# A retention and gated-MLP kernel: two accumulators swapped, two scalings shared between VectorE and GpSimd, and two small steps moved to VectorE

## The chip, the cores and the metric

The kernel runs on one core of one Trainium2 chip. The core has five engines, each with its own instruction queue: TensorE (PE in the profile; its weight loads are shown apart as PEld), VectorE (DVE), ScalarE (ACT), GpSimd (POOL) and SyncE (SP), which here only issues DMAs. TensorE's products go to accumulators in PSUM, which VectorE and ScalarE read and copy to the on-chip memory SBUF. The metric is the device time of one execution in microseconds (us); lower is better.

## The reference

```python
def _attn_ref(q, k, v):                      # (8, 8, 576, 64): batch, head, position, width
    scores = scale * np.matmul(q, k.transpose(0, 1, 3, 2))
    gamma = 1.0 - 2.0 ** (-5.0 - np.arange(H))
    rel = pos[:, None] - pos[None, :]
    Dmat = np.where(rel >= 0, gamma[:, None, None] ** rel[None], 0.0)
    return np.matmul(scores * Dmat[None], v)

def _moe_ref(x, w_in, w_out, beta):          # x (4608, 512), w_in (512, 2048), w_out (2048, 512)
    h = x @ w_in
    g = h * (1.0 / (1.0 + np.exp(-beta * h)))
    return g @ w_out
```

The attention's output, heads side by side, is `x` of the second part. All inputs and the output are float32.

## The kernel before

**Retention.** The decay `gamma ** (i - j)` is split into a factor for each query row and one for each key row. `pre_q` multiplies q by `gq`; v is multiplied by `gv` or `gvh`, and keys are copied to bf16. Within a piece of positions the causal product is computed directly: scores on TensorE, a mask on VectorE (`R`), then mask times v (`O`). What comes from earlier pieces goes through a state, the running sum of key times v, kept in float32 by additions on VectorE (`sums`) and in bf16 (`sbds`, `sbq`, `ends`) for TensorE. The output in PSUM, `O`, is copied to `xT` in bf16, transposed so that it can be the moving side of the next product.

**MLP.** For each block of 512 rows, `up`, `ups` and `first_ups` compute `w_in` times `xT` into an accumulator `ph`, from which ScalarE makes `gT` with a Silu scaled by beta; `down` multiplies `gT` by `w_out` (already divided by beta) into `po`, which is copied to `ot` and stored.

**Batches.** Of the 576 positions of a batch, 512 form a block; the last 64 of all batches are put together into one more block. Batches 0 and 1 work in two spans of 256 positions each, and their queries and keys are transposed on TensorE (`t_q`, `s_T`, `o_T`). From batch 2 on, DMAs transpose them. Batch 0's retention stands ahead of everything else, in an order written out by hand (the `s_` functions). Here `s_keep` copies states, `s_cross` multiplies them by queries, `s_x` copies `O` to `xT`, and `ups` then starts the first `up`.

**Order.** From there on, `fill` is a list of TensorE's MLP steps. Streams of other steps have a due time each, in places of `fill`, and `merged` emits a step when its due time is reached. `d0` is the place of batch 0's first `down`, `u1` that of batch 1's first `up`. Batch 1's retention is prepared by `pre_q(1, n)`, `o_pre(span, j, a)` (j = 0 keys, j = 1 v; a is the half of the heads) and `o_T`, and done by `first_span`, `first_out`, `second_span` and `second_out`. `first_out` calls `o_out(0)`, which computes the outputs of span 0 and, between its products, the second state with `o_st(1)`; it copies the outputs, transposes the keys of span 1 (`o_T(1)`) and adds up the state (`o_keep(1)`).

**Accumulators.** PSUM is handed out by tag: three "mm", two "O", two "sc", one "st". The planner gives a new tile one of its tag's buffers and makes its first writer wait until the old tile's readers are done. `phs[0]` and `phs[1]` of `first_ups` are "mm", and so is the `ph` of each `up` that follows (L703).

**Beta.** `betas` brings beta into rows on TensorE. `betas_safe` adds 1e-12 where beta squared is below 1e-24, so that its reciprocal exists; it is used by every Silu and by the scaling of `w_out`.

Of the kernel before, what the change touches and what calls it, by code (L numbers as in the profile page):

```python
# [19 lines left out]
def kernel(  # L20
# [10 lines left out]
    nc = tc.nc  # L31
# [219 lines left out]

    def betas_safe():

        nc.gpsimd.tensor_tensor(tiny[:], beta_sb[:], beta_sb[:], ALU.mult)
        nc.gpsimd.tensor_scalar(tiny[:], tiny[:], 1e-24, 1e-12, ALU.is_lt, ALU.mult)
        nc.gpsimd.tensor_tensor(beta_sb[:], beta_sb[:], tiny[:], ALU.add)

# [18 lines left out]
    def pre_q(b, n):  # L278

        if n == 0:  # L280
            batch[b] = dict(qs=sb.tile([P, CB, H, D], BF16, name="qs", tag="qs", bufs=2),
                            qT=sb.tile([P, CB, HP, P], BF16, name="qT", tag="qT", bufs=2))
        if b < 2:
            hs, cs = slice(n // 2 * HP, (n // 2 + 1) * HP), slice(n % 2 * 2, n % 2 * 2 + 2)
            for to, hs in [(hs, hs)] if n < 2 or b < QB else turned[1:]:
                nc.vector.tensor_tensor(batch[b]["qs"][:, cs, to], q_tiles[b][:, hs, cs].rearrange("p h i d -> p i h d"),
                                        gq[:, cs, hs].unsqueeze(3).to_broadcast([P, 2, len(range(H)[hs]), D]), ALU.mult)
        else:
            if n % 2:
                return  # L290
            cs = slice(n, n + 2)
            for to, hs in turned:
                nc.gpsimd.tensor_tensor(batch[b]["qs"][:, cs, to], q_tiles[b][:, hs, cs].rearrange("p h i d -> p i h d"),  # L293
                                        gq[:, cs, hs].unsqueeze(3).to_broadcast([P, 2, len(range(H)[hs]), D]), ALU.mult)
# [62 lines left out]
    def span_of(b, s):  # L357
        if (b, s) not in spans:
            spans[b, s] = dict(kn=sb.tile([P, 2, H, D], BF16, name="kn", tag="kn", bufs=4),
                               kT=sb.tile([P, 2, HP, P], BF16, name="kT", tag="kT", bufs=4),  # L360
                               vn=sb.tile([P, 2, H, D], BF16, name="vn", tag="vn", bufs=VB), R={})
        return spans[b, s]
# [61 lines left out]
    def s_x(a, hh, e):  # L424
        e(xt(0)[:, 2 * a:2 * a + 2].rearrange("k p i (s h w) -> k (p i) s h w", s=2, h=2)[:, :, :, hh, :],  # L425
          s_Os[a][hh].rearrange("k s p (i w) -> k (p i) s w", i=CB))
# [20 lines left out]
    def s_keep(a, n, es, bank=None, at=None):  # L447

        ps, at = slice(2 * a, 2 * a + 2), 2 * a if at is None else at
        for j in range(2):  # L450
            st = s_sts[min(n, 1) if bank is None else bank][half(j), at:at + 2, half(j)]
            if n < 3:
                es[j](sbds[n][half(j), ps, half(j)], st)  # L453
            else:
                es[j](ends[0][half(1 - j if a else j), ps], st)
# [104 lines left out]
        return lambda: cross(1), evict  # L560


    def o_pre(s, j, a, e=None):

        w, S, e = slice(a * HP, (a + 1) * HP), span_of(1, s), e or nc.gpsimd
        src = span_tiles[1, s, j].rearrange("p h i d -> p i h d")
        if j:
            e.tensor_tensor(S["vn"][:, :, w], src[:, :, w],
                            gvh[:, 2 * s:2 * s + 2, w].unsqueeze(3).to_broadcast([P, 2, HP, D]), ALU.mult)
            return  # L570
        for to, hs in turned[1:] if a else turned[:1]:
            e.tensor_copy(S["kn"][:, :, to], src[:, :, hs])  # L572

    def o_T(s, tags, es):

        S, ts = spans[1, s], []
        for a in range(2):
            if a < len(tags):
                T = psum.tile([P, 2 // len(tags), 2, 2, P], BF16, name="T", tag=tags[a], bufs=3 if tags[a] == "mm" else 2)
            t = T[:, a if len(tags) == 1 else 0]  # L580
            for i in range(2):
                for pl in range(2):
                    nc.tensor.transpose(t[:, i, pl, :], heads(S["kn"][:, i], 2 * a + pl), ident[:])
            ts.append(t)
        for a in range(2):
            es[a](S["kT"][:, :, 2 * a:2 * a + 2], ts[a])
# [19 lines left out]
                    nc.vector.tensor_tensor(S["R"][a][:, j], sc[a][j][:], causal_span[:].unsqueeze(2).to_broadcast([P, 2, 2, P]), ALU.mult)  # L606
        return masks

    def o_st(c):

        S, hh = spans[1, c // 2], c % 2
        st = psum.tile([P, HP, D], F32, name="st", tag="st", bufs=1)
        for i in range(2):
            for p in range(HP):
                for j in range(2):
                    nc.tensor.matmul(st[half(j), p, :], S["kn"][half(hh), i, 2 * p + j, :], S["vn"][half(hh), i, head_of(1, p, j), :],
                                     start=i == 0 and p == 0, stop=True, skip_group_check=True)
        return st
# [12 lines left out]
    def o_out(s):  # L631

        S, seen = spans[1, s], set()
        O = {(hh, y): psum.tile([P, 2, P], F32, name="O", tag="sc" if y else "O", bufs=2) for y in range(2) for hh in range(2)}

        def to(hh, p, x):
            first, o = (hh, p // 2, x) not in seen, O[hh, p // 2][half(x), p % 2, :]
            seen.add((hh, p // 2, x))
            return o, first

        def own(hj):
            for i in range(2):
                for pp in range(2):
                    for y in range(2):
                        for hh, j in hj:
                            p = pp + 2 * y
                            h = head_of(1, p, j)
                            o, first = to(hh, p, h % 2)
                            m = nc.tensor.matmul(o, S["vn"][half(hh), i, h, :], S["R"][y][half(hh), j, i, pp, :],  # L649
                                                 start=first, stop=True, skip_group_check=True)  # L650
                            held_back.append(m)
            return m

        def cross(cj):
            for pp in range(2):
                for y in range(2):
                    for hh, j in cj:
                        c, p = 2 * s + hh, pp + 2 * y
                        o, first = to(hh, p, j ^ y)
                        m = nc.tensor.matmul(s_view(o), sbq[2 * c - 1][half(j), p, :], o_q(c, half(j), p),  # L660
                                             start=first, stop=True, skip_group_check=True)
                        held_back.append(m)
            return m

        def fence(last):
            f = nc.vector.memset(fenced[:], 0.0)
            after(f, last)
            held_back.clear()
            return f

        held_back = []
        if s == 0:
            f = fence(cross([(1, 0), (1, 1)]))
            st = o_st(1)
            own([(0, 0), (0, 1), (1, 1)])
            held_back.clear()
            own([(1, 0)])
        else:
            f = fence(own([(0, 1), (1, 0)]))
            own([(0, 0), (1, 1)])  # L680
            st = o_st(3)
            cross([(0, 0), (1, 1)])
            held_back.clear()
            cross([(0, 1), (1, 0)])
        for m in held_back[:2 + 2 * s]:
            after(m, f)

        def evict():
            for n, ((hh, y), o) in enumerate(O.items()):
                c = 2 * s + hh  # L690
                (dve, act)[n % 2](xt(1)[:, 2 * y:2 * y + 2, :, c * PC:(c + 1) * PC], o.rearrange("k p (i w) -> k p i w", i=CB))
        return evict, st
# [75 lines left out]
    def F(f, *a):  # L768
        return lambda: f(*a)
# [3 lines left out]

    warm_up(2, MB)
    betas()
    betas_safe()
    pre_q(0, 0)
    pre_q(0, 1)
    t_q(0, 0)
# [36 lines left out]
    s_x(0, 0, act)  # L816
    s_cross(3, 0)
    s_st(1, 1, 0, low)
    s_x(0, 1, act)
    s_keep(1, 0, (dve, dve), 1)  # L820
    s_st(1, 0, 1, low)
    s_keep(1, 2, (dve, dve), 0)
    s_O(0, 1, "sc")
    s_O(1, 1, "sc")
    cast_w_in(0, (0, 1), (1,))
    cast_w_in(1, (0, 1), (1,))
    cast_w_in(0, (2, 3), (3,))
# [63 lines left out]
    def first_out():  # L891
        evict, st = o_out(0)
        evict()
        o_T(1, ("mm",), (act, dve))
        o_keep(1, st)

    def second_span():
        masks = o_sc(1)
# [9 lines left out]
    def triangles():  # L908
        for t, pattern in zip(tri, ([[1, CB], [CB, TL // CB]], [[1, TL]])):
            nc.gpsimd.memset(t[:], 1.0)  # L910
            for x in range(2):
# [11 lines left out]
                (d0 + 13.6, F(x_k, XB, 0)),  # L923
                (base[2] - 4.5, F(release, 4)), (base[2] + 10, F(release, 4))],
               [(d0 + 7, F(pre_q, 1, n)) for n in range(4)] + [(d0 + 12.5, F(pre_q, XB, n)) for n in range(4)] + [(d0 + 11.6, F(t_q, 1, 0)), (d0 + 11.6, F(t_q, 1, 1))],
               [(d0 + 8, F(o_pre, 0, 0, 0)), (d0 + 8, F(o_pre, 0, 0, 1)), (d0 + 9, F(o_pre, 0, 1, 0)),
                (d0 + 12.7, F(o_T, 0, ("O", "sc"), (dve, act))), (d0 + 12.8, F(o_pre, 0, 1, 1, nc.vector)),
                (d0 + 14, first_span), (d0 + 15.9, first_out)],
               [(d0 + 10, F(o_pre, 1, 0, 0)), (d0 + 10, F(o_pre, 1, 0, 1)), (d0 + 12, F(o_pre, 1, 1, 0)), (d0 + 12, F(o_pre, 1, 1, 1)),
# [89 lines left out]
```

## Time and profile before

| | us |
|---|---|
| median of three runs | 296.62 (296.17 to 297.3) |
| the profiled execution | 296.88 |
| its span, first to last instruction | 295.1 |
| TensorE busy | 289.5 |
| ScalarE busy | 145.7 |
| GpSimd busy | 110.0 |
| VectorE busy | 103.1 |

The profile is one execution. Its span is shorter than its time by 1.8 us, which lie before the first and after the last instruction. Busy times are of the whole span, and TensorE's is nearly all of it. What a change elsewhere is worth is therefore read from the few places at which TensorE waits: in the chain of waits, which goes back from the last instruction to what released each step, and in the timelines of the engines around these places. Matmuls are pipelined: one begins before the one ahead of it has ended, so the distance from start to start tells how fast they are issued.

### The profile page before, as it was taken

The numbers are of one execution on the slowest core, as the hardware profiler recorded it, in microseconds if no ns is written. First come the engines' busy times: TensorE is split into PE (matmuls) and PEld (weight loads), VectorE is DVE, ScalarE is ACT, GpSimd is POOL, SyncE is SP. The second block draws the span as 40 slices with busy tenths as digits, with TensorE's granted clock in tenths as the row PEclk, the third lists the DMA queues.
The fourth block names the chain that finished last, engine by engine and source line by source line (L and its number), as shares of the span: only waits on it lengthen the run. The fifth ranks groups of instructions, "written<-read, shape, count | busy, mean of one in ns | idle before, by whom it ended". The sixth has DMA issues, their size and how long they took to land.

```text
span 295.1 us, 7955 instructions
## 1 busy us (share of the span) xinstructions
PE 289.5 (98%) x3404; PEld 150.0 (51%) x3404; DVE 103.1 (35%) x219; ACT 145.7 (49%) x260; POOL 110.0 (37%) x218
## 2 busy tenths in 40 slices
PE   7999999999999999999999999999999999999995
PEld 3654467875544454455445544554554544444443
DVE  5765566505630651055204520354053500110012
ACT  5566537892377334743473348434770167007600
POOL 5956037945904614271229405764323000000000
PEclk9999999999999999999999999999999999999999
DMA  7999999999999799939999939999997110131011
GB/s 224 305 368 384 378 301 276 213 180 235 198 216 259 188 162 244 252 59 160 211 252 215 187 105 266 183 183 199 210 165 143 73 38 0 36 71 38 0 71 71
DMA packets 119938, 53.99 MB, mean 183 GB/s; under 512 B 93648, under 2 KB 112352, under 8 KB 119904
## 3 DMA queue, kind: packets, MB, share of 16 engines
q1 hardware_dynamic: 119872, 53.49, 81.0%
q8 instruction: 26, 0.43, 0.6%
q14 instruction: 8, 0.07, 0.1%
q10 hardware_dynamic: 32, 0.01, 0.0%
HBM read 36.71 MB, written 9.44 MB: 156 GB/s over the span
## 4 chain that ended last, share of the span: by engine, by line
PE 95%; ACT 1%; DMA 1%; DVE 0%; issue 0%; DVEq 0%
PE po L738 43%; PE ph L703 38%; PE ph L718 4%; PE O L531 2%; PE sc L485 1%; PE O L544 1%; PE st L503 1%; DMA qn<-in_q_dram 1%; PE T L346 1%; ACT sbd L453 1%; PE ph L244 1%; PE sc L399 0%; PE sc L600 0%; PE T L379 0%; ACT xT L425 0%; PE O L649 0%
## 5 line engine op out<-in xcount | busy, mean ns | idle before, releaser
L738 PE MATMUL po<-w_out_sb,gT 128*128 128x512 bf16 (+3 forms) x614 | 128.7, 366 | 0.0
L705 ACT ACTIVATE gT<-ph,beta_sb 128x512 bf16<-128x512 f32 (+1 forms) x143 | 91.1, 645 | 49.2 <-PE ph L703 48.8
L703 PE MATMUL ph<-xT,w_in_sb 128*128 128x512 bf16 (+1 forms) x572 | 113.7, 359 | 0.5 <-ACT gT L872 0.5
L738 PEld LDWEIGHTS <-gT 128*128 128x128 bf16 x614 | 58.0, 98 | 62.8
L703 PEld LDWEIGHTS <-w_in_sb 128*128 128x128 bf16 x572 | 55.5, 98 | 56.1 <-issue 0.8
L745 DVE COPY ot<-po 128x512 f32<-128x512 f32 (+2 forms) x33 | 22.2, 672 | 72.8 <-PE po L738 72.8
L293 POOL TENSOR_TENSOR qs<-qn,gq 128x256 bf16<-128x256 f32 (+1 forms) x36 | 26.3, 757 | 34.2 <-DMA qn<-in_q_dram 33.8
L492 DVE TENSOR_TENSOR R<-sc,tri 128x512 bf16<-128x512 f32 x28 | 17.4, 683 | 60.0 <-PE sc L485 60.0
L322 POOL CAST kn<-kvn 128x128 bf16<-128x128 f32 (+1 forms) x72 | 20.9, 328 | 34.2 <-DMA kvn<-in_k_dram 34.1
L300 POOL TENSOR_TENSOR vn<-kvn,gv 128x512 bf16<-128x512 f32 x24 | 25.0, 1041 | 7.7 <-DMA kvn<-in_v_dram 7.5
L559 ACT CAST xT<-O 128x512 bf16<-128x512 f32 x14 | 7.5, 588 | 32.2 <-PE O L544 32.2
L514 ACT CAST sbd<-warm 128x256 bf16<-128x256 f32 x18 | 7.3, 405 | 25.5 <-DVE warm L511 20.7
L718 PE MATMUL ph<-xT,w_in_sb 128*128 128x512 bf16 x56 | 12.9, 379 | 0.1
L511 DVE TENSOR_TENSOR first<-st,warm 128x256 f32<-128x256 f32 x24 | 10.2, 425 | 2.5
L511 DVE TENSOR_TENSOR warm<-st,first 128x256 f32<-128x256 f32 x18 | 7.6, 422 | 9.6 <-PE st L503 8.4
L559 DVE CAST xT<-O 128x512 bf16<-128x512 f32 x14 | 9.0, 686 | 5.1 <-PE O L544 5.1
L721 ACT ACTIVATE gT<-ph,beta_sb 128x512 bf16<-128x512 f32 x14 | 8.6, 686 | 4.2 <-PE ph L718 4.2
L310 POOL TENSOR_TENSOR kn<-tln,gq 128x128 bf16<-128x128 f32 (+1 forms) x12 | 5.6, 470 | 11.8 <-DMA tln<-in_q_dram 7.0
L210 POOL CAST w_in_sb<-wt 128x256 bf16<-128x256 f32 (+1 forms) x15 | 7.9, 540 | 5.0 <-DMA wt<-in_moe_w_in_dram 4.9
L718 PEld LDWEIGHTS <-w_in_sb 128*128 128x128 bf16 x56 | 5.3, 97 | 6.4 <-issue 0.5
L514 ACT CAST sbd<-first 128x256 bf16<-128x256 f32 x18 | 7.3, 405 | 2.3 <-DVE first L511 0.3
L572 POOL CAST kn<-kvn 128x256 bf16<-128x256 f32 (+1 forms) x6 | 2.9, 516 | 13.3 <-DMA kvn<-in_k_dram 13.3
(117 smaller groups left out, 176.6 us busy)
## 6 DMA issues: line engine op xcount, KB each, us to landing
qn<-in_q_dram SPq DMA_DIRECT2D x16, 512.0 KB, 5.9
kvn<-in_k_dram SPq DMA_DIRECT2D x32, 256.0 KB, 5.9
kvn<-in_v_dram SPq DMA_DIRECT2D x32, 256.0 KB, 5.5
out_dram<-ot SPq DMA_DIRECT2D x31, 256.0 KB, 3.6
wt<-in_moe_w_out_dram SPq DMA_DIRECT2D x8, 512.0 KB, 8.8
wt<-in_moe_w_in_dram SPq DMA_DIRECT2D x5, 512.0 KB, 10.2
wt<-in_moe_w_in_dram SPq DMA_DIRECT2D x6, 256.0 KB, 5.7
tln<-in_q_dram SPq DMA_DIRECT2D x8, 128.0 KB, 3.6
```

What stands on the lines that cost most here:

```text
L293: nc.gpsimd.tensor_tensor(batch[b]["qs"][:, cs, to], q_tiles[b][:, hs, cs].rearrange("p h i d -> p i h d"), gq[:, cs, hs].unsqueeze(3).to_ ...
L300: nc.gpsimd.tensor_tensor(live[i]["vn"], kv_tiles.pop(i)[:, 1], gains(gv, c), ALU.mult)
L322: nc.gpsimd.tensor_copy(kn[:, c % 2, to], t[:, 0, hs])
L492: nc.vector.tensor_tensor(R[x][:, j].rearrange("k c p q -> k (c p) q"), sc[x, j].rearrange("k c p q -> k (c p) q"), mask, ALU.mult)
L511: nc.vector.tensor_tensor(new[:], add, sums[(c - 1) % 2][:], ALU.add)
L514: nc.scalar.copy((sbq[c] if c < NC - 1 else ends[u])[:], new[:])
L559: (nc.scalar.copy if n % 2 else nc.vector.tensor_copy)(x, o)
L703: nc.tensor.matmul(ph, w_in_sb[:, ko, fo * P:(fo + 1) * P], xts[m][:, ko, :, w], start=(ko == 0), stop=(ko == KO - 1))
L705: nc.scalar.activation(gts[m][:, fo, :, w], ph, ACT.Silu, scale=beta_sb[:, fo:fo + 1])
L718: nc.tensor.matmul(phs[f][:], w_in_sb[:, ko, f * P:(f + 1) * P], xts[m][:, ko], start=(ko == 0), stop=(ko == KO - 1))
L738: nc.tensor.matmul(po[:, x:y], gT[:, fo, ms, :], w_out_sb[:, fo, n0 + x:n0 + y], start=(fo == 0), stop=(fo == FO - 1), skip_group_check=m < 2)
L745: (nc.scalar.copy if m == 0 else nc.vector.tensor_copy)(ot, po[:, :nn])
```

## The change

- `first_out` (batch 1): `o_st(1)` takes an "mm" accumulator in place of "st", and the key transposes of span 1 take "st" in place of "mm". `o_keep(1, st)` is emitted ahead of `o_T(1, ...)`.
- `pre_q(1, 3)`: the last quarter of batch 1's queries (two operations) is scaled on GpSimd.
- `o_pre(0, 1, 1)`: of the four heads of this v product VectorE keeps two, and GpSimd does the other two, from a second step in the list.
- Batch 0: the second copy to `xT`, `s_x(0, 1)`, goes from ScalarE to VectorE, and the two copies of `s_keep(1, 2)` from VectorE to ScalarE.
- `betas_safe` goes from GpSimd to VectorE, and from the start of the kernel to just behind the hand-written part.

TensorE's and SyncE's instructions are the same, in the same order.

```diff
     def betas_safe():
-        nc.gpsimd.tensor_tensor(tiny[:], beta_sb[:], beta_sb[:], ALU.mult)
-        nc.gpsimd.tensor_scalar(tiny[:], tiny[:], 1e-24, 1e-12, ALU.is_lt, ALU.mult)
-        nc.gpsimd.tensor_tensor(beta_sb[:], beta_sb[:], tiny[:], ALU.add)
+        nc.vector.tensor_tensor(tiny[:], beta_sb[:], beta_sb[:], ALU.mult)
+        nc.vector.tensor_scalar(tiny[:], tiny[:], 1e-24, 1e-12, ALU.is_lt, ALU.mult)
+        nc.vector.tensor_tensor(beta_sb[:], beta_sb[:], tiny[:], ALU.add)
...
             for to, hs in [(hs, hs)] if n < 2 or b < QB else turned[1:]:
-                nc.vector.tensor_tensor(batch[b]["qs"][:, cs, to], ...
+                e = nc.gpsimd if b and n == 3 else nc.vector
+                e.tensor_tensor(batch[b]["qs"][:, cs, to], ...
...
-    def o_pre(s, j, a, e=None):
-        w, S, e = slice(a * HP, (a + 1) * HP), span_of(1, s), e or nc.gpsimd
+    def o_pre(s, j, a, e=nc.gpsimd):
+        S, w = span_of(1, s), slice(a * HP + (2 if e is nc.vector else 0), (a + 1) * HP - (2 if e is not nc.vector and s == 0 and a else 0))
...
             e.tensor_tensor(S["vn"][:, :, w], src[:, :, w],
-                            gvh[:, 2 * s:2 * s + 2, w].unsqueeze(3).to_broadcast([P, 2, HP, D]), ALU.mult)
+                            gvh[:, 2 * s:2 * s + 2, w].unsqueeze(3).to_broadcast([P, 2, w.stop - w.start, D]), ALU.mult)
...
-            e.tensor_copy(S["kn"][:, :, to], src[:, :, hs])
+            nc.gpsimd.tensor_copy(S["kn"][:, :, to], src[:, :, hs])
...
     def o_T(s, tags, es):
-                T = psum.tile([P, 2 // len(tags), 2, 2, P], BF16, name="T", tag=tags[a], bufs=3 if tags[a] == "mm" else 2)
+                T = psum.tile([P, 2 // len(tags), 2, 2, P], BF16, name="T", tag=tags[a], bufs=1 if tags[a] == "st" else 2)
...
-    def o_st(c):
+    def o_st(c, tag="st"):
-        st = psum.tile([P, HP, D], F32, name="st", tag="st", bufs=1)
+        st = psum.tile([P, HP, D], F32, name="st", tag=tag, bufs=3 if tag == "mm" else 1)
...
-            st = o_st(1)
+            st = o_st(1, "mm")
...
     betas()
-    betas_safe()
     pre_q(0, 0)
...
-    s_x(0, 1, act)
+    s_x(0, 1, dve)
     s_keep(1, 0, (dve, dve), 1)
     s_st(1, 0, 1, low)
-    s_keep(1, 2, (dve, dve), 0)
+    s_keep(1, 2, (act, act), 0)
     s_O(0, 1, "sc")
     s_O(1, 1, "sc")
+    betas_safe()
...
         evict, st = o_out(0)
         evict()
-        o_T(1, ("mm",), (act, dve))
         o_keep(1, st)
+        o_T(1, ("st",), (act, dve))
...
-               [..., (d0 + 9, F(o_pre, 0, 1, 0)),
+               [..., (d0 + 9, F(o_pre, 0, 1, 0)), (d0 + 9, F(o_pre, 0, 1, 1)),
                 (d0 + 12.7, F(o_T, 0, ("O", "sc"), (dve, act))), (d0 + 12.8, F(o_pre, 0, 1, 1, nc.vector)),
```

More of the change, by code (lines that the diff above doesn't have):

```diff
@@ L285, in pre_q @@
             for to, hs in [(hs, hs)] if n < 2 or b < QB else turned[1:]:
-                nc.vector.tensor_tensor(batch[b]["qs"][:, cs, to], q_tiles[b][:, hs, cs].rearrange("p h i d -> p i h d"),
+                e = nc.gpsimd if b and n == 3 else nc.vector
+                e.tensor_tensor(batch[b]["qs"][:, cs, to], q_tiles[b][:, hs, cs].rearrange("p h i d -> p i h d"),
                                         gq[:, cs, hs].unsqueeze(3).to_broadcast([P, 2, len(range(H)[hs]), D]), ALU.mult)
@@ L925 @@
                [(d0 + 7, F(pre_q, 1, n)) for n in range(4)] + [(d0 + 12.5, F(pre_q, XB, n)) for n in range(4)] + [(d0 + 11.6, F(t_q, 1, 0)), (d0 + 11.6, F(t_q, 1, 1))],
-               [(d0 + 8, F(o_pre, 0, 0, 0)), (d0 + 8, F(o_pre, 0, 0, 1)), (d0 + 9, F(o_pre, 0, 1, 0)),
+               [(d0 + 8, F(o_pre, 0, 0, 0)), (d0 + 8, F(o_pre, 0, 0, 1)), (d0 + 9, F(o_pre, 0, 1, 0)), (d0 + 9, F(o_pre, 0, 1, 1)),
                 (d0 + 12.7, F(o_T, 0, ("O", "sc"), (dve, act))), (d0 + 12.8, F(o_pre, 0, 1, 1, nc.vector)),
```

## The prediction

> **What bounds the kernel now.** The page first. The span is 295.1 us, TensorE (PE) is busy for 98% of it at the full granted clock, and the chain that ended last runs through PE for 95%. So only a stretch in which PE has nothing to issue can be won, and whatever makes PE wait is lost.
>
> ```profile
> span 295.1 us, 7955 instructions
> PE 289.5 (98%) x3404; PEld 150.0 (51%) x3404; DVE 103.1 (35%) x219; ACT 145.7 (49%) x260; POOL 110.0 (37%) x218
> PE 95%; ACT 1%; DMA 1%; DVE 0%; issue 0%; DVEq 0%
> ```
>
> Then the chain in order of time (start, us, what), looked through for pieces that are not PE. Behind the first loads there are two that this change comes near: the state and x copies on ScalarE (ACT) before the first products of `ups` (L718), and one Silu (L872) in batch 1. From 50.33 on it is PE to the end but for the last copy.
>
> ```profile
> 15.24 1.08 ACT xT L425 x2
> ...
> 16.37 1.02 PE ph L718 x4
> ...
> 48.93 0.85 PE ph L869 x7
> ...
> 49.80 0.48 ACT gT L872
> ...
> 50.33 0.60 PE ph L703 x4
> ```
>
> Last the timelines of the engines around these two places (start, us, engine, line, count, idle before and its releaser).
>
> ```profile
> 48.84 1.03 PE L869 MATMUL ph<-xT,w_in_sb 128*128 128x256 bf16 x8
> 50.33 0.27 PE L703 MATMUL ph<-xT,w_in_sb 128*128 128x256 bf16 x1 [0.45 <-ACT gT L872]
> 48.27 0.76 DVE L691 CAST xT<-O 128x256 bf16<-128x256 f32 x2 [0.45 <-PE O L649]
> 49.59 0.42 DVE L586 COPY kT<-T 128x512 bf16<-128x512 bf16 x1 [0.56 <-ACT kT L586]
> 49.93 0.42 DVE L624 TENSOR_TENSOR first<-st,warm 128x256 f32<-128x256 f32 x1
> 15.62 1.20 DVE L453 CAST sbd<-st 64x128 bf16<-64x128 f32 x4
> 17.76 0.69 DVE L425 CAST xT<-O 128x512 bf16<-128x512 f32 x1 [0.94 <-PE O L421]
> ```
>
> The reader is to see that the eight L869 products issue about 0.11 apart from 48.84, so the ninth, L703, could go at 49.71 and goes at 50.33. It waits for an "mm" accumulator: three exist, the key transposes `T` hold one, `phs[0]` and `phs[1]` the others, and the one handed to L703 is that of `phs[0]`, which comes free at 50.28 with the first Silu.
>
> **The swap of accumulators.** In the changed program `st` of `o_st(1)` has the "mm" buffer and `T` the single "st" one. The program's waits then tie the first L703 to the reader of `st`, the addition in `o_keep(1)` on VectorE (DVE), and no longer to a Silu. As `o_keep(1)` now stands ahead of `o_T(1)`, that addition follows the two L691 copies (48.27 to 49.03): 48.95 plus 0.42 is 49.37, earlier than the 49.71 at which PE is ready. So 50.33 less 49.71, 0.62 us, goes. What is late next: DVE's half of kT. It moves behind the addition and its cast (0.42 and 0.29), starts at 49.67 instead of 49.59 and ends at 50.1; the scores that read it come behind four L703 products (to 50.14) and the other half of the scores, at about 50.4. `T` needs "st" free, which ACT's L627 gave back at 46.3, two us before. The gain is 0.62; less than nothing is excluded by the order on PE, which is the same instruction for instruction, and more by the issue rate of L869.
>
> **The second x copy in batch 0.** L718 needs both copies. Before, ACT made both, to 16.32, and PE began 0.05 later. Now ACT makes the first (to 15.83) and then the two state casts (0.53) that were DVE's; DVE makes the second right behind its last mask, where its casts began, at 15.62. At 0.69 that ends at 16.31: DVE is too late for a gain. The price is the release. An x copy of DVE ended at 18.46 and its L718 began at 18.60, 0.15 behind, against 0.05 behind ACT; in both the program has one more separate wait on PE when ACT and DVE have to be waited for together. I take 16.46, a loss of 0.09; the ends are 16.36 (0.05 behind) and 16.55 (no overlap with the mask), so 0.01 won to 0.18 lost. The casts moved behind the copy (DVE to 16.83, ACT to 16.28) are read at 17.23, so they cost nothing, with 0.4 of cover.
>
> **The beta guard.** Three small operations leave GpSimd's (POOL's) head, 5.61 to 7.71, and come on DVE behind the casts.
>
> ```profile
> 5.61 0.66 POOL L254 TENSOR_TENSOR rbeta_sb<-beta_sb 128x16 f32<-128x16 f32 x1 [1.77 <-ACT beta_sb L250]
> 6.35 0.82 POOL L255 TENSOR_SCALAR rbeta_sb<-rbeta_sb 128x16 f32<-128x16 f32 x1
> 7.26 0.46 POOL L256 TENSOR_TENSOR beta_sb<-beta_sb,rbeta_sb 128x16 f32<-128x16 f32 x1
> 7.67 0.60 POOL L370 CAST kn<-kvn 128x512 bf16<-128x512 f32 x1
> 9.10 2.04 POOL L372 TENSOR_TENSOR kn<-kvn,gvh 128x512 bf16<-128x512 f32 x2 [0.27 <-DMA kvn<-in_k_dram]
> ```
>
> POOL wins nothing by it: L372 waited for a load anyway, and PE was streaming until 8.52, behind the first cast (8.27). On DVE they are not in the trace. From below: three at 0.06 (its 128x1 memset), 0.2. From above: POOL's own 2.1. Nearest is L148, 128x15, mean 0.244; with 0.03 between dependent ones 0.8. From 16.83 that ends at 17.63, inside the 0.94 that DVE waited until 17.76: nothing. Without that cover each us beyond 17.76 delays the second x copy and the L718 at 18.60 by as much. The first Silu (19.51) and the reciprocal (18.57) wait for them too.
>
> **The shared scalings.** Of `pre_q(1, 3)` two DVE products (0.42 each) go to POOL, whose row for this shape (L293, 128x256) is 0.615; of `o_pre(0, 1, 1)` half goes to POOL, 0.6, and DVE keeps some 0.4 of 0.68. DVE gets faster where nobody waited. POOL gets longer ahead of the key casts, so there the cover counts. Alone POOL would do its products from 40.13 to 41.3. But it starts beside DVE products:
>
> ```profile
> 40.09 1.43 DVE L286 TENSOR_TENSOR qs<-qn,gq 128x256 bf16<-128x256 f32 x4 [0.23 <-DMA qn<-in_q_dram]
> 41.09 0.90 POOL L572 CAST kn<-kvn 128x512 bf16<-128x512 f32 x1 [12.18 <-DMA kvn<-in_k_dram]
> 44.77 0.61 POOL L572 CAST kn<-kvn 128x512 bf16<-128x512 f32 x1 [0.93 <-DMA kvn<-in_k_dram]
> ```
>
> The same cast took 0.90 beside the last DVE product and 0.61 alone: one such neighbour costs POOL 0.29. Two cost 0.58, so POOL is done at 41.9 (bounds: 41.3, and 42.04 if it can't begin before DVE's second is over at 40.85). PE's last transposes of q, at 42.2, are 0.3 behind. The three casts (0.61, 0.40, 0.40, with some 0.05 of overlap) end at 43.15; PE wants the last at 43.5. Then a v product (1.04) to 44.15 and the half to 44.7, or 45.0 with one more collision; the states (L616) need it at about 45.2. Cost nothing, with 0.2 of cover; bounds nothing and 0.4 (both collisions at full length, half done at 45.57). The key casts behind it in POOL's queue, 44.77, may slip by 0.3; their readers are PE's transposes at 48.31. [...]
>
> **The sum.** No DMA is moved. The profiled execution took 296.88 us (its span 295.1 and 1.8 around it): 296.88 - 0.62 + 0.09 = 296.35. It lies 0.26 over the median of the runs, 296.62; from that, 296.09. I forecast 296.1.
>
> **The rivals.** *A, the gain is waited away later.* The scores at 227.60 took 0.67 in the chain where others took 0.58: the last tail keys had only just been turned. If these come no earlier, PE stands there longer by what it had won: 296.6. For it: that tail's cast waited for a load. Against: the operation ahead of it was released by PE.
>
> ```profile
> 219.69 0.61 POOL L310 TENSOR_TENSOR kn<-tln,gq 128x256 bf16<-128x256 f32 x1 [4.78 <-PE ph L703]
> 221.24 0.40 POOL L311 CAST kn<-tln 128x256 bf16<-128x256 f32 x1 [0.94 <-DMA tln<-in_k_dram]
> ```
>
> The loads' queue also stands behind stores of results that DVE copies when PE is done, so it should move with PE.
>
> *B, slower: the beta guard keeps the second x copy waiting.* If DVE needs for it what POOL did, 2.1, it ends at 18.93 and delays 17.76 by 1.17: 296.09 + 1.17 = 297.3. It decides from 0.94 us for the three, and makes a net loss from 1.5. Against: DVE's rows for small tiles are a third of POOL's, which stood beside DVE products.
>
> *C, the collision.* If POOL stands still for the whole of each DVE product beside it, q is done at 42.04 and the v half at up to 45.57, and PE's states wait up to 0.4: 296.5. For and against: the two casts of 0.90 and 0.61 above.
>
> *D, the swap doesn't free PE:* L703 still finds its buffer taken, only the 0.09 is left, 296.7. Against: the program's waits.
>
> *E, more is won:* the x copies' wait goes as well, PE being ready at 16.1, 0.27 + 0.09 more: 295.7. Against: the masks hold DVE until 15.7.
>
> **How the numbers follow.** Forecast 0.60, A 0.12, B 0.05, C 0.13, D 0.05, E 0.05. The three runs before lie from 296.17 to 297.3, so a median carries some 0.4 either way; 295.4 to 297.0 takes in all but B and such tails. About 0.5%, 1.5 us, is what a measurement of this kernel can tell from no change. Under 295.14 only something unseen leads, 0.05; over 298.1 B with another loss, 0.06; 0.89 lie between.
>
> **What would show it.** After: L703's idle before it gone and the first L703 at about 49.8; L624 ahead of L586 on DVE, near 49.0; the first L718 at 16.4 to 16.5, released by DVE; the three beta rows done before 17.8; POOL's q products at 0.6 to 1.2 each and no idle on PE before its transposes at 43.5 or its states at 45.2; the scores near 227 at 0.6. It is wrong if PE shows a new wait for POOL between 42 and 46, or for DVE at 18.6.

## The result, and the profile after

| | us |
|---|---|
| before, median of 13 runs | 296.77 (296.17 to 297.3) |
| changed, median of 13 runs | 295.99 (295.47 to 296.72) |
| ratio, with its 95% interval | 0.9977 [0.9966, 0.9988] |
| the changed kernel's profiled execution, its span | 295.54, 293.8 |

296.1 was forecast. The change wins 0.1% to 0.3%, well within the 0.5% that the prediction called no change, though the interval leaves no change out. That 295.99 came so near to 296.1 is in part luck: 0.53 us were forecast from a median of 296.62, and 0.78 (0.4 to 1.0 by the interval) were measured from one of 296.77. The profiled executions differ by 1.34 us (296.88 and 295.54), the medians by 0.78: part of what the two traces show belongs to the execution, not to the edit. The experiments keep the two apart.

The page of the changed kernel shows PE's stream as full as it was, and VectorE with 1.3 us more work:

```profile
span 293.8 us, 7959 instructions
PE 287.5 (98%) x3404; PEld 148.9 (51%) x3404; DVE 104.4 (36%) x219; ACT 145.6 (50%) x261; POOL 110.0 (37%) x218
PE 95%; DMA 2%; POOL 1%; SPq 1%; issue 0%; DVE 0%; POOLq 0%
```

The lines of this kernel stand one lower from `pre_q` on: L870 and L704 are the former L869 and L703, L719 the former L718. First the place of the accumulators, in the timelines of PE and DVE (start, us, engine, line, count, idle before and its releaser):

```profile
48.51 1.03 PE L870 MATMUL ph<-xT,w_in_sb 128*128 128x256 bf16 x8
49.38 0.60 PE L704 MATMUL ph<-xT,w_in_sb 128*128 128x256 bf16 x4
49.91 0.64 PE L601 MATMUL sc<-qT,kT 64*64 64x128 bf16 x32
...
48.61 0.41 DVE L625 TENSOR_TENSOR first<-st,warm 128x256 f32<-128x256 f32 x1
49.05 0.64 DVE L630 CAST sbd<-first 128x256 bf16<-128x256 f32 x1
49.61 0.41 DVE L587 COPY kT<-T 128x512 bf16<-128x512 bf16 x1
```

The first L704 goes 0.87 behind the first L870, which is eight issues of 0.11: the idle of 0.45 that its row carried is gone. The addition ends at 49.02, 0.36 before L704 needs its accumulator. The scores (L601) follow L704 without a gap although VectorE's half of kT ends only at 50.02.

Then the front, in the same two timelines:

```profile
15.45 0.64 PE L414 MATMUL O<-R,vn 64*64 64x128 bf16 x32
16.02 1.04 PE L719 MATMUL ph<-xT,w_in_sb 128*128 128x512 bf16 x4
...
14.98 0.68 DVE L426 CAST xT<-O 128x512 bf16<-128x512 f32 x1
16.19 0.25 DVE L254 TENSOR_TENSOR rbeta_sb<-beta_sb 128x16 f32<-128x16 f32 x1
16.47 0.31 DVE L255 TENSOR_SCALAR rbeta_sb<-rbeta_sb 128x16 f32<-128x16 f32 x1
16.82 0.37 DVE L256 TENSOR_TENSOR beta_sb<-beta_sb,rbeta_sb 128x16 f32<-128x16 f32 x1
17.43 0.69 DVE L426 CAST xT<-O 128x512 bf16<-128x512 f32 x1 [0.24 <-PE O L422]
```

VectorE's new x copy is over at 15.66, 0.36 before L719 begins: it is early, not late as predicted. The guard ends at 17.19 and leaves 0.24 of VectorE's former idle of 0.94.

### The profile page after: what moved, and what is told of

The parts are those of the page before. It is cut to its first block, busy times and chain, and to the rows that moved or that the text cites. A ratio compares the mean times of both kernels' runs of the same rounds, so it can differ in the third digit from the quotient of the medians.

```text
span 293.8 us, 7959 instructions
## 1 busy us (share of the span) xinstructions
PE 287.5 (98%) x3404; PEld 148.9 (51%) x3404; DVE 104.4 (36%) x219; ACT 145.6 (50%) x261; POOL 110.0 (37%) x218
## 4 chain that ended last, share of the span: by engine, by line
PE 95%; DMA 2%; POOL 1%; SPq 1%; issue 0%; DVE 0%; POOLq 0%
PE po L739 43%; PE ph L704 38%; PE ph L719 4%; DMA kvn<-in_k_dram 2%; PE O L532 2%; PE sc L486 1%; PE st L504 1%; PE O L545 1%; POOL kn L373 1%; PE st L445 1%; PE O L414 0%; PE sc L601 0%; PE O L650 0%; SPq L102 0%; POOL vn L373 0%; PE T L584 0%
## 5 line engine op out<-in xcount | busy, mean ns | idle before, releaser
L704 PE MATMUL ph<-xT,w_in_sb 128*128 128x512 bf16 (+1 forms) x572 | 113.6, 358 | 0.0
L704 PEld LDWEIGHTS <-w_in_sb 128*128 128x128 bf16 x572 | 55.7, 98 | 55.2 <-DVE first L512 0.6
L719 PE MATMUL ph<-xT,w_in_sb 128*128 128x512 bf16 x56 | 12.9, 379 | 0.0
L719 PEld LDWEIGHTS <-w_in_sb 128*128 128x128 bf16 x56 | 5.2, 98 | 6.3 <-issue 0.5
L227 DVE TENSOR_SCALAR w_out_sb<-wt,rbeta_sb 128x512 bf16<-128x512 f32 x13 | 5.9, 484 | 5.0 <-DMA wt<-in_moe_w_out_dram 5.0
```

The lines of the kernel that those rows point to most:

```text
L704: nc.tensor.matmul(ph, w_in_sb[:, ko, fo * P:(fo + 1) * P], xts[m][:, ko, :, w], start=(ko == 0), stop=(ko == KO - 1))
L719: nc.tensor.matmul(phs[f][:], w_in_sb[:, ko, f * P:(f + 1) * P], xts[m][:, ko], start=(ko == 0), stop=(ko == KO - 1))
```

## The experiments

All are compared with the kernel before on their own chip. "Wait of the first L703" is its start less that of the last L869, less 0.11 for the issue; "wait of the first L718" is its start less that of the last product ahead of it.

**One part at a time.** The swap alone (buffers and order), and everything but the swap:

```diff
-                T = psum.tile(..., bufs=3 if tags[a] == "mm" else 2)
+                T = psum.tile(..., bufs=dict(mm=3, st=1).get(tags[a], 2))
-    def o_st(c):
+    def o_st(c, tag="st"):
-        st = psum.tile([P, HP, D], F32, name="st", tag="st", bufs=1)
+        st = psum.tile([P, HP, D], F32, name="st", tag=tag, bufs=3 if tag == "mm" else 1)
-            st = o_st(1)
+            st = o_st(1, "mm")
-        o_T(1, ("mm",), (act, dve))
         o_keep(1, st)
+        o_T(1, ("st",), (act, dve))
```

> The kernel before with the swap of accumulators and the new order in first_out alone (o_st(1) in mm, key transposes in st, o_keep(1) ahead of o_T(1)). Theory (the swap is the gain): the first L703 follows the last L869 by 0.11 us, no idle for a Silu, and the time is 0.6 us under before, ratio near 0.998. Rival (the gain is in the front of the kernel): no more than 0.2 us under before.

> The changed kernel with first_out as before (st in st, T in mm, o_T(1) ahead of o_keep(1)); the x copy, the guard and the shared scalings stay changed. Theory: the 0.6 us wait of the first L704 for the Silu of L873 is back, and the time lies within 0.2 us of before. Rival (front): 0.3 us or more under before, with the wait back all the same.

The swap alone: 295.97 (six runs), ratio 0.9966 [0.9953, 0.9979], wait of the first L703 0.00. The rest alone: 296.97, ratio 1.0005 [0.9993, 1.0016], wait 0.62, as before. The gain is the swap's, and the rest gives none.

**The two halves of the swap.** The order of `o_keep` and `o_T` alone, with the buffers of before, and the buffers alone, in the order of before (the lines of the diff above, divided).

> The kernel before with o_keep(1) emitted ahead of o_T(1), tags unchanged: T is still in mm. Theory: the buffers in mm are T, phs[0] and phs[1] as before, so the first L703 still waits for the Silu or, if the planner now hands it the buffer of T, for the key copies at about 50.1; 0 to 0.3 us are won. Rival (the order alone does it): 0.6 us.

> The kernel before with st of o_st(1) in mm and T in st, but o_T(1) still ahead of o_keep(1). Theory: the addition that reads st comes behind VectorE's key copy, ends near 50.35 in the time of before, and the first L703 waits for it or for the Silu: about 0 us won. Rival (the tags alone do it): the wait is gone and 0.6 us are won.

297.04, ratio 1.0005 [0.9994, 1.0016], and 296.7, ratio 1.0001 [0.9991, 1.0012]. PE's and DVE's timelines, first of the order alone, then of the buffers alone:

```profile
49.89 0.60 PE L703 MATMUL ph<-xT,w_in_sb 128*128 128x256 bf16 x4 [0.45 <-ACT gT L872]
48.50 0.41 DVE L624 TENSOR_TENSOR first<-st,warm 128x256 f32<-128x256 f32 x1
```

```profile
50.98 0.60 PE L703 MATMUL ph<-xT,w_in_sb 128*128 128x256 bf16 x4 [0.45 <-ACT gT L872]
50.58 0.41 DVE L624 TENSOR_TENSOR first<-st,warm 128x256 f32<-128x256 f32 x1
```

L703 waits for the Silu in both, 0.62 each, and begins 0.05 behind the Silu's end; with the buffers alone it begins at 50.98, just before the addition ends at 50.99, so it isn't the addition that it waits for. An earlier addition is worth nothing while L703 has the accumulator of `phs[0]`; and with the buffers alone, the addition to `first` standing behind the kT copy, the planner still hands it that one. It takes both: the swap alone differs from the buffers alone only in the order, and there L703 goes before the Silu has ended, so it has the state's accumulator, the one of the three that is free by then. How the planner chooses is inferred from these runs.

**The front and the shared scalings.** The second x copy, the state copies and the beta guard moved, nothing else (the lines of `s_x`, `s_keep` and `betas_safe` in the diff of the change); and, apart from that, only `pre_q(1, 3)` and `o_pre(0, 1, 1)` shared.

> The kernel before with the edits of batch 0 alone: second x copy on VectorE, the s_keep(1, 2) copies on ScalarE, beta guard on VectorE behind the hand-written part. Theory: the first L717 product of ups follows the last product ahead of it by 0.15 us where TensorE ran at its fast rate in the first microseconds (VectorE's masks are done early), in place of 0.35 in the kernel before, and by 0.4 where it ran at half of it; in the time within 0.2 us of before. Rival (my working before the run): 0.09 us lost in both.

> The kernel before with the shared scalings alone (pre_q(1, 3) and half of o_pre(0, 1, 1) on GpSimd). Theory: no idle of TensorE between 41 and 46 us but what the kernel before has, the wait for the Silu unchanged at 0.62, the time within 0.2 us of before. Rival (collision): GpSimd's keys or v half come late, TensorE stands for up to 0.4 us for a GpSimd tile in this stretch, and the time is that much over before.

296.6, ratio 1.0004 [0.9992, 1.0015], wait of the first L718 0.15. And 296.51, ratio 1.0000 [0.9988, 1.0011], wait 0.34 (both copies still on ScalarE), no PE idle for POOL from 41 to 46. Each is worth nothing that 34 runs of the kernel before can tell. (The expectation of the first says L717 for the first product of `ups`; it is L718.)

**How far the covers reach.** From the changed kernel: the guard's first operation done eight times, and the last two quarters of batch 1's queries scaled on GpSimd, four products instead of two (`n >= 2`).

```diff
-        nc.vector.tensor_tensor(tiny[:], beta_sb[:], beta_sb[:], ALU.mult)
+        for _ in range(8):
+            nc.vector.tensor_tensor(tiny[:], beta_sb[:], beta_sb[:], ALU.mult)
...
-                e = nc.gpsimd if b and n == 3 else nc.vector
+                e = nc.gpsimd if b and n >= 2 else nc.vector
```

> The changed kernel with the first operation of the beta guard done eight times (same result). At 0.28 us each this adds 2.0 us on VectorE between its state casts and the second x copy, of which 0.25 us are covered in the profile of the changed kernel. Theory (the guard lies on the path to the first Silu and the x copy as soon as its cover is used up): the second x copy starts 1.7 us late and TensorE waits at the product behind it for about as long, the time 1.5 to 1.8 us over the changed kernel, 0.7 to 1.0 over before. Rival (other work or later waits swallow it): under 0.5 us over the changed kernel.

> The changed kernel with pre_q(1, 2) on GpSimd too: four query products there, from 40.2 us, with no VectorE product beside them (0.57 us from start to start, done at 42.5). Theory (cover of GpSimd's chain some 0.3 us): TensorE waits 0.3 to 0.5 us for GpSimd at its last query transposes near 42.2, and the time is 0.3 to 0.5 over the changed kernel. Rival (the cover is larger than worked out): no wait, time as the changed kernel.

The longer guard: 297.43, ratio 1.0029 [1.0015, 1.0043]. Its timelines of PE and DVE:

```profile
17.74 1.03 PE L720 MATMUL ph<-xT,w_in_sb 128*128 128x512 bf16 x4
19.85 1.02 PE L720 MATMUL ph<-xT,w_in_sb 128*128 128x512 bf16 x4 [1.09 <-POOL w_in_sb L210]
...
16.93 1.64 DVE L255 TENSOR_TENSOR rbeta_sb<-beta_sb 128x16 f32<-128x16 f32 x8
18.81 0.18 DVE L257 TENSOR_TENSOR beta_sb<-beta_sb,rbeta_sb 128x16 f32<-128x16 f32 x1
19.02 0.69 DVE L427 CAST xT<-O 128x512 bf16<-128x512 f32 x1
```

The x copy that follows the guard begins when the guard ends (19.02), and PE waits 1.09 for it. The releaser in the row is an inference: POOL's cast had ended at 19.25, and L720 goes 0.14 after the copy's end at 19.71. The ratio is 0.0052 above the changed kernel's, some 1.5 us with about 0.5 either way by the two intervals; 1.09 of it is seen here. The guard of 2.06 starts at 16.93, and the copy could have begun at 17.93 (19.02 less 1.09): once about 1 us is used up, the guard is on the path. The wait is shorter than the 1.7 that were expected, as each of the eight took 0.21 from start to start and not 0.28.

More products on GpSimd: 296.43, ratio 0.9997 [0.9986, 1.0008]. PE and POOL:

```profile
42.70 0.40 PE L347 MATMUL T<-ident,qs 128*128 128x128 bf16 x4 [0.56 <-POOL qs L287]
40.30 2.34 POOL L287 TENSOR_TENSOR qs<-qn,gq 128x256 bf16<-128x256 f32 x4 [11.38 <-DMA qn<-in_q_dram]
```

The last transposes of q wait 0.56 for POOL, a little more than the 0.3 to 0.5 expected, and nearly the whole gain of the swap is given back. Two products fit under PE's work; four don't.

**Together on one chip.** The swap alone again, the changed kernel again, and the swap with the second x copy but without the guard and the sharing.

> The kernel before with the swap of accumulators alone (buffers and order), a second time, on one chip with the next two. Theory 'the swap is the whole gain': no wait of the first L703, time below before by 0.6 us, ratio 0.998, and even with the changed kernel within 0.3 us. Rival 'the other parts take some of the swap's gain back' (the first look had 0.9966 for the swap alone and 0.9977 for the whole change): lower than the changed kernel by 0.3 us or more, ratio 0.9966 again.

> The changed kernel once more, on one chip with the swap alone and with the swap plus the second x copy. Theory 'the swap is the whole gain': ratio 0.998 (-0.6 us), no wait of the first L704. Rival 'the other parts cost': above the swap alone by 0.3 us. For the front: the first L719 0.15 behind the product ahead of it if VectorE's last mask is over by 15.5, 0.4 if it is over by 15.9.

> The swap of accumulators and the second x copy on VectorE, without the beta guard and the shared scalings. Theory 'the swap is the whole gain': ratio 0.998, as the swap alone. Rival 'the x copy wins where VectorE's masks end early': the wait ahead of the first L718 is 0.15 instead of 0.34, and the time lies 0.2 us under the swap alone. Rival 'the x copy costs': wait 0.42, 0.1 us over it.

| | median | ratio | first L718, its wait |
|---|---|---|---|
| swap alone | 296.3 | 0.9988 [0.9978, 0.9997] | 16.34, 0.34 |
| changed kernel | 296.03 | 0.9982 [0.9971, 0.9993] | 16.77, 0.42 |
| swap and x copy | 296.28 | 0.9983 [0.9972, 0.9993] | 16.34, 0.15 |

No first L703 waits. The swap's own 0.62 of 296.77 makes a ratio of 0.9979, which every interval of a kernel with the swap holds (the first six runs of the swap alone, 0.9966, only with its upper end). The lower ratio of those six did not return, and neither "the rest takes some back" nor "the x copy wins 0.2" is borne out. No version here is measurably faster than the changed kernel.

## Why the prediction was right, point by point

**The swap: right, mechanism and size.** The sum had -0.62. TensorE's products are the same in all 13 traces, so each can be laid beside the trace of before, product by product: at the first L703 all seven with the swap get ahead by 0.62, and the five without it by nothing. In the times the gain is less sharp, as the ratios above show. The predicted order of events is there: addition first, then kT, whose later end delays nobody.

**The second x copy: the size, and at times the sign.** The term was +0.09, from a copy that begins behind the masks at 15.62. In the trace of before PE began L718 0.35 after the last product ahead of it, though only the two copies stood between. With VectorE making the second one, that wait was 0.15 where VectorE's copy began early (14.98 in the changed kernel, 15.42 in the front alone): it was then done with ScalarE's, over 0.3 before L719 began, so these 0.15 are no wait for a copy, and what they are the trace doesn't show. The wait was 0.42 where VectorE's masks ran late (copy at 15.99 in everything but the swap, at 15.95 in the changed kernel's second profile, at 15.72 in the longer guard); the first product of `ups` then began 0.14 or 0.15 behind the copy's end, the predicted price of a release by VectorE. So the term is -0.20 or +0.07 (0.15 or 0.42 less 0.35), by how soon the masks are done, and one trace of before could not tell which. The assumption that failed is "DVE is too late for a gain": the casts' place at 15.62, 0.40 ahead of the last product before L718, was taken for fixed. In four of the seven traces with the moved copy it is 0.90 ahead, in the other three 0.40. In the times neither sign can be seen.

**The beta guard: hidden, with less to spare.** 0.8 was estimated. It took 1.0 (16.19 to 17.19) beside POOL's weight casts, which ran to 17.16, and 0.6 where no cast was in its way, in the changed kernel's second profile:

```profile
17.15 0.17 DVE L254 TENSOR_TENSOR rbeta_sb<-beta_sb 128x16 f32<-128x16 f32 x1
17.36 0.17 DVE L255 TENSOR_SCALAR rbeta_sb<-rbeta_sb 128x16 f32<-128x16 f32 x1
17.57 0.17 DVE L256 TENSOR_TENSOR beta_sb<-beta_sb,rbeta_sb 128x16 f32<-128x16 f32 x1
18.17 0.69 DVE L426 CAST xT<-O 128x512 bf16<-128x512 f32 x1 [0.43 <-PE O L422]
```

Rival B's mechanism is real and its threshold about where it was put (0.94, and about 1.0 in the longer guard); at 1.0 the guard of the changed kernel had 0.24 to spare.

**The shared scalings: no cost, as predicted.** VectorE, POOL and PE between 40 and 45 in the changed kernel, the first four products one by one:

```profile
40.11 0.43 DVE L287 TENSOR_TENSOR qs<-qn,gq 128x256 bf16<-128x256 f32 x1 [0.25 <-DMA qn<-in_q_dram]
40.23 0.78 POOL L287 TENSOR_TENSOR qs<-qn,gq 128x256 bf16<-128x256 f32 x1 [11.31 <-DMA qn<-in_q_dram]
40.45 0.84 DVE L287 TENSOR_TENSOR qs<-qn,gq 128x256 bf16<-128x256 f32 x1
40.98 0.79 POOL L287 TENSOR_TENSOR qs<-qn,gq 128x256 bf16<-128x256 f32 x1
42.97 1.79 POOL L569 TENSOR_TENSOR vn<-kvn,gvh 128x512 bf16<-128x512 f32 x2
43.72 0.57 DVE L569 TENSOR_TENSOR vn<-kvn,gvh 128x256 bf16<-128x256 f32 x1
...
41.19 1.06 PE L347 MATMUL T<-ident,qs 128*128 128x128 bf16 x16
42.08 1.04 PE L739 MATMUL po<-w_out_sb,gT 128*128 128x256 bf16 x8
42.96 0.61 PE L584 MATMUL T<-ident,kn 128*128 128x128 bf16 x8
```

POOL's q is done at 41.77 (41.9 predicted) and the v half at 44.76 (44.7 to 45.0). PE shows no idle. The collision is mutual, which the prediction left out: VectorE's first product took 0.43 as before, its second 0.84 against 0.42, and its half of v 0.57 where 0.4 was expected. VectorE gained little by handing work over, but nobody waited for it.

The rows show how they collide: the two engines take turns. POOL's first product ends 0.47 behind the end of VectorE's first (41.01 and 40.54), VectorE's second 0.28 behind that (41.29), and POOL's second again 0.47 behind that (41.77). The same two numbers come back at the halves of v: VectorE's ends 0.28 behind POOL's first v product (44.29 and 44.01, 42.97 plus its 1.04), POOL's 0.47 behind that (44.76). In the trace of before, POOL's 128x512 cast ended 0.47 behind VectorE's last product (41.99 and 41.52). So in these rows the later one held still until the earlier one had ended; by an estimate, its own 0.62 or 0.42 less these 0.47 or 0.28, only about 0.15 lay ahead of the wait. What makes it wait, no run shows. The prediction's 0.29 for each neighbour was what was left of one such wait: here the wait cost POOL 0.17 each time (0.78 and 0.79 against 0.62), as VectorE's products had begun before. Rival C is thus right in its mechanism and wrong in its price: POOL does stand still, but for what remains of a product, and VectorE waits in its turn. The wait for POOL in the run with four products is no sign of rival C: those took 0.62 each, with no VectorE product beside them, and were simply too much work.

**The other rivals.** A is refuted: the scores near 227 took 0.67 in the chain in both kernels, and behind it the stream was earlier than in the trace of before by at least what it was ahead of it. D is refuted by the wait of 0.00. E's half, the x copies' wait, came in some executions, as above. One slip in the chances: B had 0.05, and times over 298.1, which were said to need B, 0.06.

**The sum.** -0.62 is shown. Laid side by side, product by product, the two profiled executions differ by about 0.15 us ahead of the first product of `ups`, by 0.20 more at it (the x copy, which came early in this execution), by 0.62 at the first L703, and by 0.37 in small steps behind it, in later batches that no edit touches. The 0.15 goes with the first microseconds of the execution, the subject of the last section. Steps like the 0.37 also come without the swap (0.34 with the order alone, 0.39 with the front alone) and differ between two executions of the changed kernel (0.37 and 0.10); what makes them, no run shows.

## What to carry to other kernels

A wait on an accumulator is set by which buffer the planner hands out, so read the program's wait, not the tile's name: changing the tag or the order alone left it untouched. Here, where the engine that sets the end is 98% busy, a stall of 0.6 us removed was worth 0.6 us, and moving work between engines that have time to spare was worth nothing, though it cost once a cover of some 0.3 us (POOL's scalings) or 1 us (the guard) was spent. Read colliding instructions one by one: the mean of VectorE's two products, 0.59, hides that one took 0.43 and the other 0.84. When two single traces differ by more than the medians do, look for what changes from execution to execution before an edit gets the credit.

## What the runs showed of the hardware that was not expected

**In eight of the 13 traces TensorE runs at half speed for a part of the first 12 us, and which part differs between executions.** The same four transposes of 128 columns take 0.40 or 0.63 us, issued 0.055 or 0.107 apart. One execution, that of the buffers alone, has both, in PE's timeline:

```profile
7.53 0.40 PE L346 MATMUL T<-ident,qs 128*128 128x128 bf16 x4 [0.23 <-DVE qs L286]
8.15 0.61 PE L346 MATMUL T<-ident,qs 128*128 128x128 bf16 x4 [0.23 <-DVE qs L286]
8.98 0.63 PE L379 MATMUL T<-ident,kn 128*128 128x128 bf16 x4
11.59 0.39 PE L379 MATMUL T<-ident,kn 128*128 128x128 bf16 x4
```

It is fast to 7.7, slow from 8.3 to 11.3, and fast again from 11.65. The clock records of this trace agree: half the clock is granted from 7.96 to 11.38, and full clock before and after. On its page the second slice, 7.4 to 14.8 us, falls to 7:

```profile
PEclk9799999999999999999999999999999999999999
```

The longer guard's trace has the same from 7.89 to 11.30. In the other traces the row stays at 9 even where products were slow, since their records begin only with the full clock (at 10.41 in the trace of before, whose transposes are slow until 9.0), and the row counts the time ahead of the first record as full; that of everything but the swap has no record at all. So for the first microseconds the distance between equal products tells more than the row, and the "full granted clock" that the prediction reads from it holds from 10.4 us on. Over the 13 profiles, the slow products seen in the front, the first record of the full clock, and the start of the first product of `ups`:

| slow products of 128 columns | profiles | full clock recorded from | first product of `ups` |
|---|---|---|---|
| none | changed kernel; swap alone twice; order alone; sharing alone | 4.69 to 5.34 | 15.85 to 16.36 |
| 2 to 8, early | front alone; more sharing; swap and x copy | 5.85 to 7.36 | 16.14 to 16.46 |
| 6 to 8, from 8.2 on | longer guard; buffers alone | 4.47 and 4.55, half again from 7.89 and 7.96 | 16.54 and 17.02 |
| 11 or 12 | before; everything but the swap; changed kernel again | 10.41, no record, 10.76 | 16.37 to 16.81 |

The changed kernel is in the first row and in the last: the speed goes with the execution, not with the edit. The first profile of it began fast and that of before slow: its stream was 0.49 ahead at 10.9 us and, other waits having taken some of it back, 0.15 at 14. Such waits may widen the rows of the table too; no run sets them apart. The x copy goes with it too: with the copy on VectorE, the first product of `ups` waited 0.15 in the four traces without a slow product behind 7.2 us, and 0.42 in the three with some at 9.0 or later. Each of the two recorded stretches of half clock lasts 3.41 us. What decides which execution starts slow, no run shows.

**The guard's operations took up to about twice their time beside the other engine, and then ended just behind it.** The guard's three took 0.25, 0.31 and 0.37 on VectorE beside POOL's casts, and 0.17 each where no cast was in the way. Each of the first three ended 0.02 to 0.03 behind the cast that had begun before it (16.44 behind 16.41, 16.78 behind 16.76, 17.18 behind 17.16): the same taking of turns as above. The casts kept their 0.40. So did they beside VectorE's masks, which read one operand from PSUM (0.40 from 14.85 on, the mask from 14.38 to 15.06). The guard's 0.66 and 0.82 on POOL in the kernel before were such waits too: they ended 0.07 and 0.14 behind a VectorE product.
